# A kernel's first ten microseconds: weights asked for before the mask, and a first convolution by head pairs

## The chip, the core and the metric

The kernel runs on one core of a Trainium2 chip. A core has five engines that run side by side, each with its own list of instructions: PE (matrix products), DVE (vector operations), ACT (functions and copies), POOL (general vector operations and some DMA requests) and SP (DMA requests). They meet at semaphores. Sixteen DMA engines move data between the chip's memory and the core's SBUF, which has 128 partitions; PE writes its products to PSUM, in eight banks, from which DVE and ACT read. The metric is the device time of one execution in microseconds (us), lower is better. The time before is 713.74 us, the median of four runs (713.51, 715.17, 713.2 and 713.98).

## The reference

The input `x` has 8 sequences of 4096 tokens with 192 channels, in 8 heads of 24. A causal convolution of length 7 mixes neighbouring tokens with one softmax-normalised filter per head; a two-layer network with the activation h cos(h) follows:

```python
w = softmax(weight, axis=-1)                       # weight: [8 heads, 7 taps]
x_pad = concatenate([zeros((B, 6, D)), x], axis=1)
conv[b, s, h, g] = sum_k w[h, k] * x_pad[b, s + k, h * 24 + g]
h = conv.reshape(32768, 192) @ w_in                # w_in: [192, 2048]
out = (h * cos(h)) @ w_out                         # w_out: [2048, 192]
```

## The kernel before

**Tiling.** The 32768 tokens are 64 tasks of 512 tokens (`t` in the loop at L480); two tasks make a unit of 1024 (`u`). A unit's x is loaded as fp32 (`x_f`, L75), cast to bf16 (`x_bf`, L183), convolved on PE with banded matrices (L194), copied from PSUM to `ct` with each 64 channels twice (L207, L209, L258), and turned by a DMA transpose (L267) to `cT`, channels on partitions. Then, per task, eight blocks of the first product go to PSUM (`mm1`, L395, three `h` tiles of two banks each, used in turn), ACT takes the cosine (L402), DVE multiplies (`g`, L406), and PE adds up the second product (`mm2_step`, L439) in two further banks, `o_ps0` and `o_ps1`.

**Order.** No scheduler decides: every engine runs its instructions in the order in which the kernel writes them. From task 0 on PE's and ACT's orders are written out by hand as strings (L468 to L476), in which `h3` is the fourth block of `mm1` and `m5` five steps of the second product. Waits are put in by the framework from what the instructions read and write.

**The opening.** The lines up to L381 prepare task 0, and the change lies there.

- *The filters.* `weight` is loaded as 4 rows of 2 heads (`w_row`, L63). POOL makes `quarter` (L112 to L115), and a matmul with it (L122) spreads the four rows over the four quarters of the partitions: partitions 32q to 32q+31 hold head pair q. The softmax runs on that (L147 to L156) and ends in `wn`. Before and after this matmul, `keep_warm` has PE multiply zeros (L108).
- *The mask.* `mask[p, e, k]` is one where e + k = p + 6. POOL makes it on 32 partitions (L130, L131); DVE makes one copy to a further quarter and ACT two (L136). `prod = mask * wn` (L306) and a sum over k (L309) give `diag`: 38 columns of each band matrix.
- *The bands.* Sixteen small copies (L320; DVE, POOL and ACT by the letters "DPDPDPADPDPADPAD") put `diag` into `band`, the 8 heads' banded 128x256 matrices, which DVE has zeroed (L134). The copies go head pair by head pair.
- *Requests.* POOL asks for w_in in two halves, cast to bf16 on the way (L85), after the mask and before zeroing a row of `x_bf` (L139) and making the unit matrix `ident` (L141, L142). SP asks for x's first 512 tokens at once, and for its next ones when `diag` is done (L311 to L315).
- *First convolution and turning.* `conv_first` convolves the 512 tokens in two halves of two 128-token blocks: for each half, 8 heads by 2 (a block and the one before it), 16 matmuls of 48 columns into one bank. ACT copies out half 0, DVE half 1 (L343). Then SP asks for w_out (L96). `turn_first` turns each block on PE by a product with `ident` (L358), and ACT and DVE copy it to `cT` (L361). Task 0's first block, in two parts `h0a` and `h0b`, needs blocks 0 and 1 of `cT`, and blocks 2 and 3.
- *The second half of unit 0.* `conv_rest` convolves it during task 0 (`r` in PE's order), DVE and ACT copy it out (L207), and a DMA transpose turns it for task 1.

Of the kernel before, what the change touches and what calls it, by code (L numbers as in the profile page):

```python
# [8 lines left out]
FP32 = mybir.dt.float32  # L9
BF16 = mybir.dt.bfloat16  # L10
AF = mybir.ActivationFunctionType
ALU = mybir.AluOpType
# [4 lines left out]
def kernel(  # L17
# [66 lines left out]
    def load_w(t):  # L84
        nc.gpsimd.dma_start(out=w[64 * t : 64 * t + 64].rearrange("p k j f -> p k (j f)"), in_=w_src[t])  # L85
# [20 lines left out]
    def keep_warm(n, bank=idle):  # L106
        for _ in range(n):
            nc.tensor.matmul(out=bank, lhsT=zero[:, 0:128], rhs=zero, start=True, stop=True)  # L108
# [5 lines left out]
                            channel_multiplier=-32)  # L114
    nc.gpsimd.affine_select(out=quarter, in_=quarter, compare_op=ALU.is_ge, fill=0.0, base=31, pattern=[[-1, 128]],  # L115
                            channel_multiplier=32)
    scrap = consts.tile([128, 1], FP32)
    nc.scalar.activation(out=scrap, in_=one, func=AF.Exp)
    keep_warm(3)
# [5 lines left out]

    xb0 = xbf_pool.tile([128, UB + 1, D], BF16, name="x_bf")

    E = 32 + K - 1
    mask = consts.tile([128, E, K], BF16)
    nc.gpsimd.memset(mask[0:32], 0.0)  # L130
    nc.gpsimd.affine_select(out=mask[0:32], in_=mask[0:32], compare_op=ALU.not_equal, fill=1.0, base=1 - K,  # L131
                            pattern=[[1, E], [1, K]], channel_multiplier=-1)
    band = consts.tile([128, H, 256], BF16)
    nc.vector.memset(band, 0.0)  # L134
    for q, copy in enumerate((nc.vector.tensor_copy, nc.scalar.copy, nc.scalar.copy)):
        copy(out=mask[32 * q + 32 : 32 * q + 64], in_=mask[0:32])  # L136
    for t in range(2):
        load_w(t)
    nc.gpsimd.memset(xb0[:, 0, :], 0.0)  # L139
    ident = consts.tile([128, 128], BF16)  # L140
    nc.gpsimd.memset(ident, 0.0)  # L141
    nc.gpsimd.affine_select(out=ident, in_=ident, compare_op=ALU.not_equal, fill=1.0, base=0, pattern=[[1, 128]],  # L142
                            channel_multiplier=-1)
    wn = consts.tile([128, HQ, K], BF16)

    wmax = consts.tile([128, HQ, 1], FP32)
# [2 lines left out]
    nc.vector.tensor_tensor(out=wexp, in0=w_bc, in1=wmax.to_broadcast([128, HQ, K]), op=ALU.subtract)  # L149
    nc.scalar.activation(out=wexp, in_=wexp, func=AF.Exp)  # L150
    nc.scalar.activation(out=scrap, in_=one, func=AF.Sin)
    wsum = consts.tile([128, HQ, 1], FP32)
    nc.vector.tensor_reduce(out=wsum[:, :, 0], in_=wexp, axis=mybir.AxisListType.X, op=ALU.add)
    winv = consts.tile([128, HQ, 1], FP32)
# [56 lines left out]
    def ring_banks():  # L211
        h = h_pool.tile([128, 2, T], FP32, name="h")
        return [h[:, 0, :], h[:, 1, :]]

    def o_banks():
        return [o_pools[b].tile([128, T], FP32, name="o_ps%d" % b) for b in range(2)]
# [66 lines left out]
    def mend_edges(u):  # L283
# [12 lines left out]
        for j in (1, 2):  # L296
# [6 lines left out]
    cast_unit(0, 0, NB, nc.scalar.copy)  # L303

    prod = consts.tile([128, HQ, E, K], BF16)
    nc.vector.tensor_tensor(out=prod, in0=mask.rearrange("p (o e) k -> p o e k", o=1).to_broadcast([128, HQ, E, K]),  # L306
                            in1=wn.rearrange("p h (o k) -> p h o k", o=1).to_broadcast([128, HQ, E, K]), op=ALU.mult)
    diag = consts.tile([128, HQ, E], FP32)
    summed = nc.vector.tensor_reduce(out=diag, in_=prod, axis=mybir.AxisListType.X, op=ALU.add)  # L309
# [20 lines left out]

    def conv_first():

        banks = o_banks()
        for half in range(2):
            for h in range(H):
                for prev in range(2):
                    nc.tensor.matmul(
                        out=banks[half][:, 0 : 2 * D].rearrange("p (n k h r) -> p h n k r", n=2, k=NC, h=H)[:, h],
                        lhsT=band[:, h, 128 * prev : 128 * prev + 128],
                        rhs=bf[0][:, 2 * half + 1 - prev : 2 * half + 3 - prev, h * G : (h + 1) * G].rearrange(  # L340
                            "p n (k r) -> p n k r", k=NC),
                        start=(h == 0 and prev == 0), stop=(h == H - 1 and prev == 1), skip_group_check=True)
            m = copies[half](out=ct_tiles[0][:, 2 * half : 2 * half + 2].rearrange("p n k t w -> p (n k) t w"),  # L343
                             in_=banks[half][:, 0 : 2 * D].rearrange("p (m t w) -> p m t w", t=1, w=64).to_broadcast(
                                 [128, 2 * NC, 2, 64]))
        tc.add_manual_dep(nc.sync.nop().ins, m.ins.name, sync_dep, reason="order of the transfers")
        load_wo(0)
        load_wo(1)

    def turn_first(half):  # L350
        for n in range(2):
            last = half and n
            ps = [o_pools[0].tile([128, T], FP32, name="o_ps0")] if last else ring_banks()
            if n == 0:
                keep_warm(2 - half, ps[1])
            ps = ps[0]
            for k in range(NC):
                nc.tensor.matmul(out=ps[:, k * 128 : (k + 1) * 128],  # L358
                                 lhsT=ct_tiles[0][:, 2 * half + n, k, :, :].rearrange("p t w -> p (t w)"), rhs=ident,
                                 start=True, stop=True, skip_group_check=True)  # L360
            copies[n](out=cT[0][:, 2 * half + n].rearrange("p c k -> p (c k)"), in_=ps[:, 0 : NC * 128])  # L361
# [224 lines left out]
```

## Time and profile before

The profile is of one execution of 713.51 us; its span, from the first to the last instruction, is 711.8 us, and 1.7 us lie outside it.

| | busy us | share of the span |
|---|---|---|
| PE, matmuls | 701.2 | 99% |
| PE, weight loads | 537.2 | 75% |
| DVE | 646.6 | 91% |
| ACT | 590.4 | 83% |
| POOL | 301.3 | 42% |

In the opening, in us from the span's start:

| | from | to |
|---|---|---|
| POOL: `quarter` done | | 1.73 |
| POOL: mask | 1.73 | 3.02 |
| POOL: two requests for w_in | 2.99 | 4.43 |
| DVE: sum, reciprocal, product of the softmax (wsum to wn) | 4.17 | 4.74 |
| DVE: prod and diag | 4.78 | 6.00 |
| DVE: its seven band copies | 6.03 | 7.93 |
| PE: first convolution | 6.81 | 8.73 |
| task 0's first matmul | 10.47 | |
| DMA transpose of unit 0's second half, issue to landing | 16.69 | 21.99 |
| task 1's first matmul | 22.04 | |

A profile names groups of instructions by line, engine and tile, and tells what ended an engine's idle time before them. The chain of waits starts from the last instruction and goes back, at each step, to what released it. An engine that is idle off this chain costs nothing. The four runs shown lie 2 us apart.

### The profile page before, as it was taken

What the parts mean: (1) busy time and instruction counts of PE and PEld (TensorE: products, weight loads), DVE (VectorE), ACT (ScalarE), POOL (GpSimd) and SP (SyncE); (2) the same over time, 40 slices, a digit from 0 to 9 for tenths busy, and PEclk for the clock granted to TensorE, in tenths of its full rate; (3) what the DMA queues carried; (4) which work ended last, traced back from release to release, by engine and by line L of the source; (5) the groups of instructions that cost most, each with busy time, mean ns of one, the idle gap of its engine ahead of it and who ended that gap; (6) DMA issues with size and microseconds to landing.
All of it is one profiled execution on the core that took longest, in us unless ns stands there. A gap on an engine that the chain in (4) does not pass through costs nothing.

```text
span 711.8 us, 26520 instructions
## 1 busy us (share of the span) xinstructions
PE 701.2 (99%) x11829; PEld 537.2 (75%) x11829; DVE 646.6 (91%) x601; ACT 590.4 (83%) x719; POOL 301.3 (42%) x307
## 2 busy tenths in 40 slices
PE   7899999999999999999999999999999999999997
PEld 3577777777777777777777777777777777777776
DVE  7899999999999999999999999999999999999995
ACT  7888888888888888888888888888888888888774
POOL 6653335553235543445542255534355532453200
PEclk9999999999999999999999999999999999999999
DMA  8963553444653544543546544545535555513402
GB/s 214 236 145 81 141 146 102 119 118 102 147 126 107 133 99 121 146 121 101 144 86 136 145 107 114 128 92 145 147 82 138 104 117 145 126 50 91 96 25 68
DMA packets 183713, 85.25 MB, mean 120 GB/s; under 512 B 111664, under 2 KB 183216, under 8 KB 183600
## 3 DMA queue, kind: packets, MB, share of 16 engines
q1 hardware_dynamic: 182888, 82.59, 47.8%
q8 instruction: 92, 1.51, 0.8%
q0 software_dynamic: 416, 0.79, 0.7%
q14 instruction: 21, 0.17, 0.1%
q10 hardware_dynamic: 296, 0.20, 0.1%
HBM read 31.36 MB, written 25.17 MB: 79 GB/s over the span
## 4 chain that ended last, share of the span: by engine, by line
PE 96%; DVE 1%; DMA 1%; ACT 1%; issue 0%; POOL 0%; POOLq 0%; SPq 0%
PE o_ps L439 47%; PE h L395 46%; PE h L194 3%; DMA cT<-ct 1%; DVE g L406 0%; ACT cs L402 0%; PE h L439 0%; DVE band L320 0%; POOL mask L131 0%; ACT mask L136 0%; ACT ct L343 0%; PE o_ps L194 0%; DVE diag L309 0%; DVE cT L361 0%; PE h L358 0%
## 5 line engine op out<-in xcount | busy, mean ns | idle before, releaser
L406 DVE TENSOR_TENSOR g<-h,cs 128x1024 bf16<-128x1024 f32 (+1 forms) x513 | 606.2, 1220 | 30.4 <-ACT cs L402 19.8
L402 ACT ACTIVATE cs<-h 128x1024 bf16<-128x1024 f32 (+1 forms) x513 | 512.0, 1026 | 100.1 <-PE h L395 66.0
L439 PEld LDWEIGHTS <-g 64*128 64x128 bf16 x8192 | 368.9, 94 | 90.8 <-SPq L167 0.6
L439 PE MATMUL o_ps<-wo,g 64*128 64x192 bf16 x8128 | 434.3, 243 | 0.2 <-SPq L167 0.2
L395 PE MATMUL h<-cT,w 64*128 64x512 bf16 (+1 forms) x3078 | 412.4, 376 | 4.1 <-DVE g L406 2.1
L395 PEld LDWEIGHTS <-w 64*128 64x128 bf16 x3078 | 160.7, 94 | 71.6 <-issue 4.0
L292 POOL TENSOR_TENSOR edge_prod<-cT,tap 128x1008 f32<-128x1008 bf16 x30 | 67.2, 2241 | 346.4 <-DMA cT<-ct 346.4
L183 POOL CAST x_bf<-x_f 128x1728 bf16<-128x1728 f32 (+2 forms) x33 | 80.6, 2444 | 5.8 <-DMA x_f<-in_x_dram 5.4
L209 ACT CAST ct<-h 128x384 bf16<-128x384 f32 x120 | 51.7, 482 | 8.5 <-PE h L194 4.9
L450 DVE COPY o_sb<-o_ps 128x384 f32<-128x384 f32 x63 | 35.2, 558 | 23.6 <-PE o_ps L439 23.2
L258 POOL COPY ct<-ct 128x1536 bf16<-128x1536 bf16 (+1 forms) x31 | 45.7, 1473 | 2.4 <-ACT ct L209 2.4
L194 PE MATMUL h<-x_bf,band 64*128 64x192 bf16 (+1 forms) x472 | 41.0, 243 | 0.0
L297 POOL TENSOR_TENSOR edge_prod<-edge_prod 128x144 f32<-128x144 f32 x60 | 33.4, 556 | 4.7
L295 POOL TENSOR_TENSOR edge_prod<-edge_prod 128x432 f32<-128x432 f32 x30 | 30.4, 1012 | 2.4
L450 ACT COPY o_sb<-o_ps 128x384 f32<-128x384 f32 x63 | 29.8, 473 | 1.6 <-PE o_ps L439 1.6
L194 PEld LDWEIGHTS <-band 64*128 64x128 bf16 (+1 forms) x496 | 24.7, 94 | 2.1 <-issue 1.0
L298 POOL TENSOR_TENSOR cT<-edge_prod 128x144 bf16<-128x144 f32 x30 | 18.3, 610 | 2.4
L260 POOL COPY ct<-x_bf 128x192 bf16<-128x192 bf16 x60 | 19.2, 349 | 0.0
L108 PE MATMUL o_ps<-zero 128*128 128x512 bf16 x12 | 4.2, 508 | 1.3 <-DVE zero L103 1.3
L460 DVE COPY o_sb<-h 128x192 f32<-128x192 f32 x1 | 0.4, 359 | 3.7 <-PE h L439 3.7
L108 PEld LDWEIGHTS <-zero 128*128 128x128 bf16 x15 | 1.5, 115 | 2.9 <-DVE zero L103 1.3
L460 ACT COPY o_sb<-h 128x192 f32<-128x192 f32 x1 | 0.3, 319 | 3.8 <-PE h L439 3.8
(62 smaller groups left out, 43.8 us busy)
## 6 DMA issues: line engine op xcount, KB each, us to landing
out_dram<-o_sb SPq DMA_DIRECT2D x63, 384.0 KB
x_f<-in_x_dram SPq DMA_DIRECT2D x30, 768.0 KB
x_f<-in_x_dram SPq DMA_DIRECT2D x31, 96.0 KB
x_f<-in_x_dram SPq DMA_DIRECT2D x4, 384.0 KB
wo_f<-in_moe_w_out_dram SPq DMA_DIRECT2D x4, 384.0 KB
w<-in_moe_w_in_dram POOLq DMA_DIRECT2D x2, 384.0 KB, 6.2
cT<-ct SPq DMA_TRANSPOSE x32
out_dram<-o_sb ACTq DMA_DIRECT2D x2, 96.0 KB
```

Source lines behind the costliest of these rows:

```text
L183: copy(out=bf[u][:, n0 + o : n1 + o, :].rearrange("p n (h k r) -> p (n h) k r", k=NC, r=R), in_=x_tiles[u][:, n0:n1, :].rearrange("p n (h ...
L194: return nc.tensor.matmul(out=ps[i // 2][:, 0 : (n1 - n0) * 2 * G].rearrange("p (n k i r) -> p i n k r", n=n1 - n0, k=NC, i=2)[:, i % 2], ...
L209: copy(o[:, :, 0, :], i[:, :, 0, :])
L258: nc.gpsimd.tensor_copy(out=ct[:, 0:nb, :, 1, :], in_=ct[:, 0:nb, :, 0, :])
L292: nc.gpsimd.tensor_tensor(out=edge_prod, in0=window, in1=tap.rearrange("p (a b k) -> p a b k", a=1, b=1).to_broadcast([128, NC * UB, K - 1 ...
L295: nc.gpsimd.tensor_tensor(out=edge_prod[:, :, :, 0:3], in0=edge_prod[:, :, :, 0:3], in1=edge_prod[:, :, :, 3:6], op=ALU.add)
L297: nc.gpsimd.tensor_tensor(out=edge_prod[:, :, :, 0], in0=edge_prod[:, :, :, 0], in1=edge_prod[:, :, :, j], op=ALU.add)
L395: nc.tensor.matmul(out=h[:, i, n0 * 128 : n1 * 128], lhsT=w[rows, k, j, :], rhs=c[rows, m0 + n0 : m0 + n1, k, :], start=(k == 0), stop=(k ...
L402: nc.scalar.activation(out=cs[:, :, part], in_=h[:, :, part], func=AF.Sin, bias=math.pi / 2.0, scale=1.0)
L406: nc.vector.tensor_tensor(out=g_tiles[t][:, 2 * j : 2 * j + 2, part], in0=h[:, :, part], in1=cs[:, :, part], op=ALU.mult)
L439: ms.append(nc.tensor.matmul(out=o_ps[tt, b, si], lhsT=g_tiles[tt][rows, f, s * 128 : (s + 1) * 128], rhs=wo[rows, f // 2, f % 2, :], star ...
L450: copies[b](o_sb[t][:, 2 * b : 2 * b + 2, :].rearrange("p s d -> p (s d)"), o_ps.pop((t, b)))
```

## The change

Five things change, all before task 0:

- `load_w`, the two requests for w_in, goes from behind the mask to directly behind `quarter` on POOL.
- The 3-dimensional mask goes. POOL makes `shifted`, 128 rows of a unit matrix shifted by six columns. `ident` becomes a view of it. The first 32 rows by 44 columns of it are copied to the four quarters of `rows32` (POOL quarters 1 and 2, DVE 0 and 3), and `mask` becomes a view of `rows32` in which rows overlap: element (e, k) is column e + k. ACT's two mask copies and DVE's one go. DVE's two new copies stand behind the softmax's subtraction and before its sum.
- `conv_first` runs by head pairs instead of by halves: for each pair the four blocks one after the other, each into its own bank (`o_ps0`, `o_ps1` and the two banks of one `h` tile). 64 matmuls of 24 columns take the place of 32 of 48.
- Each block is copied out singly, ACT blocks 0 and 2, DVE 1 and 3.
- `turn_first` takes its banks in another order, and two of the three warming matmuls there go. The three `h` tiles are used as often as before.

The tiles that are allocated after these constants, x's among them, begin 416 bytes lower in each partition.

```diff
@@ -114,6 +114,8 @@
                             channel_multiplier=-32)
     nc.gpsimd.affine_select(out=quarter, in_=quarter, compare_op=ALU.is_ge, fill=0.0, base=31, pattern=[[-1, 128]],
                             channel_multiplier=32)
+    for t in range(2):
+        load_w(t)
     scrap = consts.tile([128, 1], FP32)
     nc.scalar.activation(out=scrap, in_=one, func=AF.Exp)
     keep_warm(3)
@@ -125,22 +127,20 @@
 
     xb0 = xbf_pool.tile([128, UB + 1, D], BF16, name="x_bf")
 
-    E = 32 + K - 1
-    mask = consts.tile([128, E, K], BF16)
-    nc.gpsimd.memset(mask[0:32], 0.0)
-    nc.gpsimd.affine_select(out=mask[0:32], in_=mask[0:32], compare_op=ALU.not_equal, fill=1.0, base=1 - K,
-                            pattern=[[1, E], [1, K]], channel_multiplier=-1)
+    shifted = consts.tile([128, 128 + K - 1], BF16)
+    nc.gpsimd.memset(shifted, 0.0)
+    nc.gpsimd.affine_select(out=shifted, in_=shifted, compare_op=ALU.not_equal, fill=1.0, base=1 - K,
+                            pattern=[[1, 128 + K - 1]], channel_multiplier=-1)
+    ident = shifted[:, K - 1 :]
     band = consts.tile([128, H, 256], BF16)
     nc.vector.memset(band, 0.0)
-    for q, copy in enumerate((nc.vector.tensor_copy, nc.scalar.copy, nc.scalar.copy)):
-        copy(out=mask[32 * q + 32 : 32 * q + 64], in_=mask[0:32])
-    for t in range(2):
-        load_w(t)
+
+    E = 32 + K - 1
+    rows32 = consts.tile([128, E + K - 1], BF16)
+    mask = bass.AP(rows32.tensor, rows32.offset, [rows32.ap[0], [0, HQ], [1, E], [1, K]])
+    for q in (1, 2):
+        nc.gpsimd.tensor_copy(out=rows32[32 * q : 32 * q + 32], in_=shifted[0:32, 0 : E + K - 1])
     nc.gpsimd.memset(xb0[:, 0, :], 0.0)
-    ident = consts.tile([128, 128], BF16)
-    nc.gpsimd.memset(ident, 0.0)
-    nc.gpsimd.affine_select(out=ident, in_=ident, compare_op=ALU.not_equal, fill=1.0, base=0, pattern=[[1, 128]],
-                            channel_multiplier=-1)
     wn = consts.tile([128, HQ, K], BF16)
 
     wmax = consts.tile([128, HQ, 1], FP32)
@@ -149,6 +149,8 @@
     nc.vector.tensor_tensor(out=wexp, in0=w_bc, in1=wmax.to_broadcast([128, HQ, K]), op=ALU.subtract)
     nc.scalar.activation(out=wexp, in_=wexp, func=AF.Exp)
     nc.scalar.activation(out=scrap, in_=one, func=AF.Sin)
+    for q in (0, 3):
+        nc.vector.tensor_copy(out=rows32[32 * q : 32 * q + 32], in_=shifted[0:32, 0 : E + K - 1])
     wsum = consts.tile([128, HQ, 1], FP32)
     nc.vector.tensor_reduce(out=wsum[:, :, 0], in_=wexp, axis=mybir.AxisListType.X, op=ALU.add)
     winv = consts.tile([128, HQ, 1], FP32)
@@ -303,7 +305,7 @@
     cast_unit(0, 0, NB, nc.scalar.copy)
 
     prod = consts.tile([128, HQ, E, K], BF16)
-    nc.vector.tensor_tensor(out=prod, in0=mask.rearrange("p (o e) k -> p o e k", o=1).to_broadcast([128, HQ, E, K]),
+    nc.vector.tensor_tensor(out=prod, in0=mask,
                             in1=wn.rearrange("p h (o k) -> p h o k", o=1).to_broadcast([128, HQ, E, K]), op=ALU.mult)
     diag = consts.tile([128, HQ, E], FP32)
     summed = nc.vector.tensor_reduce(out=diag, in_=prod, axis=mybir.AxisListType.X, op=ALU.add)
@@ -330,30 +332,31 @@
 
     def conv_first():
 
-        banks = o_banks()
-        for half in range(2):
-            for h in range(H):
-                for prev in range(2):
-                    nc.tensor.matmul(
-                        out=banks[half][:, 0 : 2 * D].rearrange("p (n k h r) -> p h n k r", n=2, k=NC, h=H)[:, h],
-                        lhsT=band[:, h, 128 * prev : 128 * prev + 128],
-                        rhs=bf[0][:, 2 * half + 1 - prev : 2 * half + 3 - prev, h * G : (h + 1) * G].rearrange(
-                            "p n (k r) -> p n k r", k=NC),
-                        start=(h == 0 and prev == 0), stop=(h == H - 1 and prev == 1), skip_group_check=True)
-            m = copies[half](out=ct_tiles[0][:, 2 * half : 2 * half + 2].rearrange("p n k t w -> p (n k) t w"),
-                             in_=banks[half][:, 0 : 2 * D].rearrange("p (m t w) -> p m t w", t=1, w=64).to_broadcast(
-                                 [128, 2 * NC, 2, 64]))
+        banks = o_banks() + ring_banks()
+        for q in range(4):
+            for n in range(NB):
+                for h in range(HQ * q, HQ * (q + 1)):
+                    for prev in range(2):
+                        nc.tensor.matmul(
+                            out=banks[n][:, 0:D].rearrange("p (k h r) -> p h k r", k=NC, h=H)[:, h],
+                            lhsT=band[:, h, 128 * prev : 128 * prev + 128],
+                            rhs=bf[0][:, n + 1 - prev, h * G : (h + 1) * G].rearrange("p (k r) -> p k r", k=NC),
+                            start=(h == 0 and prev == 0), stop=(h == H - 1 and prev == 1), skip_group_check=True)
+        for n in range(NB):
+            m = copies[n % 2](out=ct_tiles[0][:, n],
+                              in_=banks[n][:, 0:D].rearrange("p (m t w) -> p m t w", t=1, w=64).to_broadcast([128, NC, 2, 64]))
         tc.add_manual_dep(nc.sync.nop().ins, m.ins.name, sync_dep, reason="order of the transfers")
         load_wo(0)
         load_wo(1)
 
     def turn_first(half):
+        banks = o_banks() if half else None
         for n in range(2):
-            last = half and n
-            ps = [o_pools[0].tile([128, T], FP32, name="o_ps0")] if last else ring_banks()
-            if n == 0:
-                keep_warm(2 - half, ps[1])
-            ps = ps[0]
+            ps = banks[n] if half else ring_banks()
+            if not half:
+                if n == 0:
+                    keep_warm(1, ps[1])
+                ps = ps[0]
             for k in range(NC):
                 nc.tensor.matmul(out=ps[:, k * 128 : (k + 1) * 128],
                                  lhsT=ct_tiles[0][:, 2 * half + n, k, :, :].rearrange("p t w -> p (t w)"), rhs=ident,
```

## The prediction, before the result was known

> **What bounds the kernel.** I read the page first, then PE's waits by stretch, then the chain of waits up to 23 us, then each engine's timeline and the DMA share there.
>
> ```profile
> span 711.8 us, 26520 instructions
> ...
> PE 701.2 (99%) x11829; PEld 537.2 (75%) x11829; DVE 646.6 (91%) x601; ACT 590.4 (83%) x719; POOL 301.3 (42%) x307
> ```
>
> PE is busy 99% of the span, and the table of PE's waits from 40 us to the end is empty: there the order of matmuls is fixed and PE never stops. So the change, which touches the first 11 us alone, is worth exactly the shift of the moment from which PE runs without stop. The chain shows what sets that moment (start us, length us, what):
>
> ```profile
> 2.06 0.97 POOL mask L131
> ...
> 3.06 0.41 ACT mask L136
> ...
> 3.48 0.41 ACT mask L136
> ...
> 4.17 0.18 DVE wsum L153
> ...
> 4.78 0.49 DVE prod L306
> ...
> 5.29 0.72 DVE diag L309
> ...
> 8.07 0.27 PE o_ps L337 x4
> ...
> 8.36 0.81 ACT ct L343
> ...
> 9.76 0.57 DVE cT L361
> ...
> 10.47 0.67 PE h L395 x6
> ...
> 16.69 5.30 DMA cT<-ct
> ...
> 22.04 0.82 PE h L395 x6
> ```
>
> The reader should see two stretches. To 10.47 a chain of small steps: mask, softmax, band, first convolution, turning. From 11.2 to 22 DVE and ACT run task 0 (DVE is idle for 0.64 us at most between 11.79 and 23.33), then the DMA transpose of unit 0's second half, issued at 16.69, holds PE until 22.04. ACT's line says how much of that a faster transpose could give:
>
> ```profile
> 22.90 4.29 ACT L402 ACTIVATE cs<-h 128x1024 bf16<-128x1024 f32 x4 [0.82 <-PE h L395]
> ```
>
> ACT had ended task 0's last cosine at 22.08; only 0.82 us of the wait is the transpose's alone. Last, the DMA engines by stretch (columns: busy time of PE, PEld, DVE, ACT, POOL, then the clock, DMA share, GB/s):
>
> ```profile
> 3.80:4.80 1.00, 1.00 (x5) 0.33 (x3) 0.53 (x4) 0.96 (x3) 1.00 (x3) 1.00 0.36 33
> 4.80:9.20 4.40, 3.10 (x40) 1.58 (x38) 3.35 (x10) 3.50 (x7) 1.99 (x8) 1.00 0.99 148
> ...
> 10.20:18.40 8.20, 6.56 (x70) 3.40 (x69) 7.10 (x10) 7.04 (x11) 5.64 (x7) 1.00 1.11 323
> ...
> 20.20:21.70 1.50, 0.16 (x2) 0.00 (x0) 1.23 (x1) 1.50 (x4) 0.49 (x1) 1.00 1.01 230
> ```
>
> From 4.8 to 18.4 the DMA engines are full. The DMA records say with what: x's first block moves from 1.95 to 3.74, w_in's packets from 4.49 to 10.26; x's next blocks, asked for from 6.02, move nothing before 9.2, and x and w_out then fill the engines to about 18.5, with stragglers to 20. The transpose's packets run from 18.1 to 21.4 in the middle of that, with a hole.
>
> **Part 1, POOL's order.** Today: `quarter` to 1.73, mask memset and select to 3.02, the two w_in issues 2.99 to 4.43 (0.81 and 0.63), then x_bf memset, ident memset 0.22 and select 0.50. After: w_in issues 1.73 to 3.17; `shifted` memset, 0.23 by ident's row (134 columns for 128), a gap of 0.08, select 0.52: ready at 4.00. So the mask's source comes 0.98 later than today's 3.02, all of it the 1.44 of the issues less 0.46 of cheaper making. Behind it on POOL: two rows32 copies, 0.24 each by the band-copy row, to 4.5, then the x_bf memset to 4.8, which nobody needs before the first matmul at 6.8; POOL's first band copy at 6.1 stays free.
>
> **Part 2, mask copies.** Gone: ACT's two (0.41 each) and DVE's one (0.22). ACT's exponential no longer stands behind them: it goes from 3.92 to 3.74 (the subtraction ends at 3.72), and with it the table load and the x cast, 0.18 earlier; x_bf was ready at 6.75 and the last band at 7.93, so this is off the path. But DVE now waits for `shifted` in front of wsum: two 32x44 copies of 0.17 (between a 14-wide operation at 0.17 and the 32x266 copy at 0.22), 4.03 to 4.37; wsum starts at 4.39 instead of 4.17: +0.22. prod starts near 5.0, and POOL's rows, done at 4.5, don't hold it. prod and diag are the same in elements (0.48, 0.71); the overlapping view reads the same rows of seven. Bounds of this step: -0.1 (both issues at 0.63, copies 0.1 each) to +0.5 (DVE's and POOL's copies one after the other).
>
> [...]
>
> The band copies keep order and price, so the last lands at 7.93 + 0.22 = 8.15.
>
> **Part 3, convolution.** 64 matmuls of 24 columns replace 32 of 48. Start to start they stand 25 ns apart today (20 in 0.48), set by something other than 48 columns; I take 25 ns, bounds 12 and 30. A head pair is 16, 0.40. Pairs 0 to 2 go as their bands come (today 6.81, 7.2, 7.61), so the last pair starts when its band allows, at 8.29 against 8.07, and block 0 ends after its first four, as half 0 does today. Evacuation starts at 8.58 against 8.36: no gain, and no loss.
>
> **Part 4, evacuation.** One copy of 768 per engine (ACT 0.80, DVE 0.96) becomes two of 384 (0.48 and 0.56, as the L361 rows of that size). Blocks 2 and 3 are halves of one `h` tile, and in the built program DVE's copy of block 3 waits for ACT's copy of block 2; nothing like it was there before. ACT: block 0 at 8.58 to 9.06, block 2 to 9.57. DVE: block 1 8.69 to 9.25, idle, block 3 9.59 to 10.15, then block 1's turned copy 10.17 to 10.73. PE's first task matmul needs that: 10.88 instead of 10.47. Without the wait it would be 10.55. The fewer warming matmuls were beside waits and cost nothing; the clock column is 1.00 in all stretches, and PE keeps working in each 2 us here.
>
> **Part 5, w_in earlier.** Today the second weight load of task 0 starts 0.15 after the first matmul, when w_in's second half lands (last packet 10.26); six matmuls take 0.65 where two steps of 0.107 and the last one's 0.27 would be about 0.5. After, w_in is in by about 9.4: -0.15. So task 0's first cosine moves by 0.41 - 0.15 = +0.25 (bounds: -0.4 with the low mask and no wait of block 3, +0.6 with the high mask and half of the 0.15).
>
> **Part 6, the DMA queue.** w_in's packets move from 1.26 earlier, where the engines had room (share 0.36 from 3.8 to 4.8). x's first block could lose its tail: it ends at 3.74 and isn't read before 5.35, so even 1 us is covered. SP issues x's next blocks 0.22 later (they wait for diag) and w_out at 10.15 instead of 9.73 (behind the last copy of Part 4), both covered: the engines are still on w_in at 6.2, and on x's 1.28 MB (at 323 GB/s, from about 8.4) until 12.3. So everything behind w_in comes about 1.1 earlier and w_out's backlog ends near 17.3. The transpose is issued after DVE's copies, at 16.69 + 0.25 = 16.94, into a nearly empty queue. Its price there: later ones of 27 blocks begin 1.2 after the issue and move packets for 4.4, 0.163 a block, and this one landed 0.6 after its last packet; 12 blocks make 1.2 + 2.0 + 0.6 = 3.8 instead of 5.3. Bounds 3.8 and 5.3. At 3.8 it lands at 20.7 and is no longer waited for: late next is ACT (22.08 + 0.25), then DVE's last product, which frees the h buffer for task 1's third block. The 0.82 of ACT's idle is what can be had: 0.25 - 0.82 = -0.57. x for unit 2 and the second transpose follow the same queue and shift at least as far; the edge copy behind that one ended at 33.14 for a matmul at 33.39, so it must shift too.
>
> **Sum.** -0.55 on the profiled execution of 713.51 (span 711.8 and 1.7 around it): 712.96. The median, 713.74, stands 0.23 above that execution: 713.2.
>
> **Rivals.**
> (a) The transfer relief isn't had: the transpose has a hole of its own (DMA share 0.15 from 19.4 to 20.2, when nearly all of w_out had gone), which speaks for it; that later ones show none speaks against. Then only the opening counts: +0.25, 714.0; with the high bound +0.6, 714.4.
> (b) The opening gains: the mask 0.1 late only, block 3 not held (10.55 less 0.12), w_in's 0.15 in full: -0.2 - 0.82, 712.7. The wait in the built program speaks against.
> (c) Slower by one mechanism: POOL. Every us that the two issues and `shifted` take longer is a us on wsum. With the relief had, it turns the sign when the opening is 0.82 late, that is when `shifted` is ready at 4.6; to 0.2% it needs 6.0, twice the 1.44 seen and more. Price at 5.0: +0.4, 714.2.
> (d) The main loop changes: the smaller constants move all large tiles down by 416 bytes, from multiples of 64 bytes to 32 beyond. 0.2% would be 0.13 ns on each of 11270 task matmuls. The rows with such an address already (band's weight loads 95 ns, w's 94) show nothing.
>
> **How the numbers follow.** 0.2%, 1.4 us, is about what a measurement of this kernel can tell from no change; the four runs shown lie 2 us apart. The sum 0.45, (a) 0.2, (b) 0.2, (c) 0.08, (d) 0.07, split evenly by sign. The sum reads as faster beyond 0.2% in one of six by the runs' scatter, (b) in half, (d) half: 0.2. Slower beyond: (c) half, (d) half, a little of (a): 0.1. Range: (b) less the 0.5 that the lowest run lies below the median, 712.2 (its low bound, -1.2, lies inside); (a) at its high bound and a little, 714.6.
>
> **What would show it.** Right: `shifted` ready near 4.0, wsum near 4.4, DVE idle before block 3's copy, first task matmul near 10.9 with no wait for w, transpose under 4.5 and no PE wait on it. Wrong: a transpose still over 5 us, prod waiting on POOL, or any PE wait after 40 us.

## The result and the profile after

The changed kernel takes 715.68 us (median; 714.41 to 717.19) where the kernel before takes 713.49 on the same chips: the ratio is 1.0027, 95% interval 1.0022 to 1.0032. It is slower by 0.27%, 1.9 us (the medians lie 2.2 apart). The forecast was 713.2, within 712.2 to 714.6.

The profile is of an execution of 715.25 us. From its page:

```profile
span 713.6 us, 26581 instructions
...
PE 702.6 (98%) x11859; PEld 538.3 (75%) x11859; DVE 646.6 (91%) x603; ACT 589.2 (83%) x718; POOL 300.3 (42%) x307
```

PE has 30 more matmuls and 30 more weight loads: 32 of each in the first convolution, less two warming matmuls. Their busy time is 1.4 us more. From 40 us on PE again waits for nothing, so the whole difference must have arisen before, and it can be read off one mark: when DVE starts the k-th product (`g`) of the main loop, here minus before.

| product | before | after | shift |
|---|---|---|---|
| first, task 0 | 11.79 | 13.25 | +1.47 |
| ninth, the last of task 0 | 22.11 | 23.58 | +1.46 |
| tenth, the first of task 1 | 23.96 | 24.72 | +0.76 |
| fourteenth | 28.86 | 29.55 | +0.70 |
| sixteenth | 32.05 | 33.59 | +1.54 |
| last | 701.49 | 703.02 | +1.53 |

Three steps: 1.47 late at the start, 0.7 won back at 24 us, 0.8 lost again at 30 us. Each has its row in PE's waits from 8 to 60 us (us in total, times, longest):

```profile
PE h L398 <- DVE g L409: 2.4, 6, 0.6
PE o_ps L442 <- SPq L169: 1.3, 1, 1.3
PE h L398 <- DMA w<-in_moe_w_in_dram: 0.9, 1, 0.9
PE h L398 <- DMA cT<-ct: 0.4, 1, 0.4
```

The transpose's wait, 1.7 before, is 0.4: the step won. The transpose did not land earlier for that: issued 1.47 later (18.16 for 16.69), it lets PE go on at 22.21, where before PE went on at 22.04. The wait for w_in is new. The wait for SP at L169 was 0.2. L169 is the no-operation by which SP orders two halves of PE's second product (`Turn.mark`).

**The start.** The engines' timelines (start us, busy us, what; POOL, then DVE, then PE):

```profile
3.41 0.29 POOL L132 TENSOR_SCALAR_AFFINE_SELECT shifted<-shifted 128x134 bf16<-128x134 bf16 x1
...
4.12 0.17 DVE L155 TENSOR_REDUCE wsum<-wexp 128x2 f32<-128x14 f32 x1
...
9.80 0.56 DVE L346 CAST ct<-h 128x384 bf16<-128x384 f32 x1 [0.23 <-ACT ct L346]
...
10.97 0.27 PE L398 MATMUL h<-cT,w 64*128 64x256 bf16 x1 [0.21 <-DVE cT L364]
12.09 1.26 PE L398 MATMUL h<-cT,w 64*128 64x256 bf16 x15 [0.86 <-DMA w<-in_moe_w_in_dram]
```

The mask is not late: `shifted` is ready at 3.70, wsum starts 0.05 earlier than before, the last band lands at 7.94 (7.92). DVE's 0.23 before block 3 is the wait that was forecast. The first task matmul stands at 10.97 for 10.47, and the second, 0.15 behind it before, is now 1.12 behind: w_in's second half has not landed. 0.50 and 0.97 make the 1.47. But the second matmul goes by w_in alone: it follows 0.05 behind the landing of w_in's second half, at 12.04 (10.58 before), so the 0.50 is hidden behind that landing.

**The requests.** The stretches that the prediction showed, with the same columns:

```profile
3.80:4.80 1.00, 1.00 (x4) 0.30 (x2) 0.78 (x5) 0.98 (x2) 0.66 (x3) 1.00 0.91 125
4.80:9.20 4.40, 4.25 (x71) 2.33 (x69) 3.13 (x10) 2.83 (x7) 1.46 (x6) 1.00 1.01 129
...
10.20:18.40 8.20, 6.10 (x63) 3.28 (x64) 6.11 (x10) 5.61 (x10) 4.69 (x6) 1.00 1.10 304
```

The engines are busier from 3.8 to 4.8, as forecast (0.91 for 0.36), but from 4.8 to 9.2 they move less than before, 129 GB/s for 148, at the same share. The DMA records: w_in's packets run from 3.32 to 11.00 (start of the first, start of the last, here and below), where before they ran from 4.49 to 10.08, and a packet takes 244 ns on average where it took 217. Asked for 1.3 us earlier, w_in ends 0.9 later.

**The end of the chain.** Where the chain of waits before ran through the mask, the convolution and the transpose, it now comes by another way (start us, length us, what):

```profile
10.79 7.76 DMA wo_f<-in_moe_w_out_dram
18.68 1.48 POOL wo L92
20.70 5.39 DMA x_f<-in_x_dram
26.23 2.57 POOL x_bf L185
28.80 2.35 SPq L269
```

The last row is SP, busy with the second DMA transpose (unit 1's), and then PE at 31.26. Timelines of SP and PE there:

```profile
24.34 6.81 SPq L269 DMA_TRANSPOSE cT<-ct  x1
...
29.72 0.20 PE L280 MATMUL h<-wn,pick 128*128 128x7 bf16 x2
31.26 0.58 PE L442 MATMUL o_ps<-wo,g 64*128 64x192 bf16 x10 [1.34 <-SPq L169]
```

SP's no-operation stands behind the issue of the transpose, and PE's next matmul behind the no-operation. Before, that issue ran from 22.89 to 29.30, and PE lost 0.2. By stretches (DMA share and GB/s last), after:

```profile
28.00:29.00 1.00, 1.00 (x16) 0.62 (x12) 1.00 (x2) 0.51 (x1) 0.85 (x2) 1.00 0.97 211
29.00:30.00 1.00, 0.92 (x14) 0.56 (x8) 0.78 (x2) 1.00 (x2) 1.00 (x1) 1.00 2.06 69
```

and before:

```profile
29.00:30.00 1.00, 0.79 (x15) 0.55 (x13) 1.00 (x2) 1.00 (x3) 1.00 (x1) 1.00 1.27 289
30.00:31.00 1.00, 0.87 (x12) 0.56 (x13) 1.00 (x2) 0.57 (x4) 1.00 (x1) 1.00 2.50 225
31.00:32.00 1.00, 1.00 (x21) 0.69 (x17) 0.21 (x1) 1.00 (x2) 0.15 (x1) 1.00 0.07 7
```

For about a microsecond little moves (from 29 us after, from 30.7 before), and the DMA engines are counted busy twice over in the stretch where it begins. The DMA records show what stands ahead of it: a single packet of 16384 bytes on an instruction queue, at 28.78 after and at 30.29 before; 0.4 us later some twenty of the transpose's 256-byte packets, whose median is 18 ns, take 1.3 to 1.4 us each. After, this falls inside the transpose's issue, and SP can't end it; before, the issue was over.

### The profile page after: what moved, and what is told of

The parts are those of the page before. It is cut to its first block, busy times and chain, and to the rows that moved or that the text cites. A ratio compares the mean times of both kernels' runs of the same rounds, so it can differ in the third digit from the quotient of the medians.

```text
span 713.6 us, 26581 instructions
## 1 busy us (share of the span) xinstructions
PE 702.6 (98%) x11859; PEld 538.3 (75%) x11859; DVE 646.6 (91%) x603; ACT 589.2 (83%) x718; POOL 300.3 (42%) x307
## 4 chain that ended last, share of the span: by engine, by line
PE 95%; DMA 2%; DVE 1%; POOL 1%; SPq 0%; ACT 0%; issue 0%; POOLq 0%; DVEq 0%
PE o_ps L442 47%; PE h L398 45%; PE h L196 3%; DMA wo_f<-in_moe_w_out_dram 1%; DMA x_f<-in_x_dram 1%; PE h L442 0%; POOL x_bf L185 0%; SPq L269 0%; POOL wo L92 0%; PE o_ps L108 0%; DVE g L409 0%; DVE band L322 0%; ACT cs L405 0%; PE o_ps L340 0%; ACT ct L346 0%
```

## Experiments

They ask three things: which part costs (e1 to e4), whether the 16384-byte pieces do it (e7, e8, e10), and why w_in is late (e9, e13). e5, e6, e11 and e12 move other transfers. Where a ratio is given, it is to the kernel before on the same chip, with its 95% interval.

### One part undone: e1 to e4

e1 asks for w_in behind the copies of the rows, at 2.72 instead of 1.68.

```diff
-    for t in range(2):
-        load_w(t)
     scrap = consts.tile([128, 1], FP32)
...
         nc.gpsimd.tensor_copy(out=rows32[32 * q : 32 * q + 32], in_=shifted[0:32, 0 : E + K - 1])
+    for t in range(2):
+        load_w(t)
```

> The changed kernel, with the two w_in requests moved behind the rows32 copies, so that they are issued near 2.9 us as in the kernel before. Theory A (asked for early, w_in's tail mixes with x's next blocks and lands at 12.0 instead of 10.6; that is the loss): the 0.86 us wait of the first task matmul goes or falls under 0.2 us, DVE's first product moves from 13.25 to about 12.4, ratio to the kernel before about 1.000 to 1.001. Rival B (the convolution in single blocks costs it): the wait for w_in goes, but the ratio stays above 1.0015.

e2 keeps early w_in and mask, with `conv_first` and `turn_first` as before (their lines of the diff undone). e3 is both: only the mask and the addresses are changed.

> The changed kernel, with the first convolution, its copies and the turning as in the kernel before; w_in still early, mask still a view. Theory A: w_in still lands near 12.0 and holds the first task matmul, now for about 1.4 us (the matmul is ready near 10.5), ratio 1.002 to 1.003. Rival B: ratio near 1.000.

> Only the mask as a view and the identity matrix as a view are left of the change; w_in's requests and the convolution as before. Both theories: no difference to the kernel before, ratio 0.9990 to 1.0005; diag ends within 0.1 us of 6.0. A ratio above 1.001 would speak for the mask or for the lower addresses of the large tiles.

e4 is the changed kernel with x's next requests held until the last band copy:

```diff
-    tc.add_manual_dep(nc.sync.nop().ins, summed.ins.name, sync_dep, reason="order of the transfers")
-    load_unit(0, NB, UB)
...
-        three[k](out=band[...], in_=diag[...])
+        put = three[k](out=band[...], in_=diag[...])
+    tc.add_manual_dep(nc.sync.nop().ins, put.ins.name, sync_dep, reason="order of the transfers")
+    load_unit(0, NB, UB)
```

> The changed kernel, with SP's requests for x's next blocks held until the last band copy (7.95 instead of 6.05). Theory A: w_in's packets end near 10 instead of 11.2, its landing near 10.4, no wait for w_in at the first task matmul, DVE's first product near 12.4; x's later blocks come about 1 us later, which may show behind; ratio 1.000 to 1.002. Rival A2 (w_in's own packets are slow when asked for early, whatever x does): it still lands past 11.5 and the wait stays.

Measured:

| | ratio | w_in's packets, us | PE's wait for w_in | for SP near 30 us |
|---|---|---|---|---|
| e1, w_in late | 1.0015 [1.0005, 1.0024] | 4.24 to 9.79 | none | 1.63 |
| e2, convolution as before | 1.0002 [0.9993, 1.0012] | 3.54 to 9.85 | 0.2 | 0.35 |
| e3, mask alone | 1.0005 [0.9995, 1.0014] | 4.25 to 9.82 | none | 0.34 |
| e4, x held | 1.0041 [1.0026, 1.0056] | 3.51 to 10.61 | none | 1.76 |

The mask and the shift of addresses show no cost (e3; its interval ends at 0.14%). Undoing the early request wins back about half (e1), and the other half is the convolution's, but not in the opening: in e1 the first product stands at 11.83, as before (11.79), and only then does PE wait 1.63 for SP. The wait for SP goes with the new convolution: 1.3 to 1.8 in the three kernels that have it, 0.35 or less where the old one stands. e2 misses what theory A expected, a loss of 0.2 to 0.3% with early w_in alone; e9 comes back to it. e4 speaks against x's next blocks as what delays w_in: held back 2.6 us, they left w_in's end at 10.61. (PE did not wait for w_in there because its first task matmul stood at 11.67; in that profile the whole opening stood 0.7 later.) Its own loss is x, which PE then waited 1.6 for.

### The instruction stream: e7, e8 and e10

The instruction queue with the 16384-byte pieces moves 92 of them in the profile before and 93 after. For PE's 23658 and 23718 matmuls and weight loads that is 257 and 255 to a piece, so they are taken for PE's instructions. The new convolution puts 60 more instructions into the opening. e7 adds 60 to the kernel before, and nothing else:

```diff
-    keep_warm(9)
+    keep_warm(7)
+    for _ in range(32):
+        nc.tensor.matmul(out=idle[:, 0:24], lhsT=zero[:, 0:128], rhs=zero[:, 0:24], start=True, stop=True)
```

> The kernel before, with 60 more instructions on PE in the opening: two of the nine warming matmuls after the weights' row are replaced by 32 matmuls of 24 columns each, on the same bank of zeros. They end before the bands are ready, so nothing waits for them. Theory F (PE's instructions come by DMA in pieces of 16384 bytes, and a piece that comes while the transposition of unit 1 is being issued holds its packets for about 1.4 us, SP with it, and PE's second product of task 1 behind SP): the piece seen at 30.29 comes at 28.3 to 29.0, inside the issue; the issue takes 7.0 to 7.8 us instead of 6.41; PE waits 1.0 to 1.8 us on SP near 29.5; ratio 1.0010 to 1.0025. Theory G (the rest of the new convolution, its banks, its four evacuations and its later opening, makes the loss of the convolution part): PE's wait on SP stays at 0.2 to 0.4, ratio 1.000 within 0.0007.

e8 is the opposite: the changed kernel, with two blocks per matmul.

```diff
-        banks = o_banks() + ring_banks()
+        banks = o_banks()
         for q in range(4):
-            for n in range(NB):
+            for half in range(2):
                 for h in range(HQ * q, HQ * (q + 1)):
                     for prev in range(2):
...
-                            rhs=bf[0][:, n + 1 - prev, ...
+                            rhs=bf[0][:, 2 * half + 1 - prev : 2 * half + 3 - prev, ...
...
         for n in range(NB):
             m = copies[n % 2](out=ct_tiles[0][:, n],
-                              in_=banks[n][:, 0:D]...
+                              in_=banks[n // 2][:, n % 2 * D : (n % 2 + 1) * D]...
```

> The changed kernel, with the first convolution still by head pairs and still evacuated block by block, but with two blocks of 48 columns in one bank as before: 32 matmuls instead of 64, so PE's stream is as long as before (4 instructions shorter). Theory F: the piece of instructions comes at 30 or later, the second transposition's issue takes 5.8 to 6.5 us, PE's wait on SP is at most 0.4; what is left is the opening and w_in's late landing, ratio 0.9998 to 1.0012. Theory G: the four evacuations and the order by head pairs are still there, ratio 1.0018 to 1.0030, wait on SP 1.0 or more.

e10 is e8 with e1's later request.

> The changed kernel with both suspects taken out: w_in asked for behind the copies of the rows, and two blocks in one bank, so PE has no more instructions than before. What stays of the change is the mask by view, the order by head pairs and the evacuation block by block. If the 60 instructions and the early requests are all that costs: ratio 0.9995 to 1.0005, no wait of PE over 0.4 on SP or on w_in, first product of VectorE at 11.6 to 12.0. If the evacuation block by block or the order by head pairs costs too: 1.0008 or more.

e7 measured 1.0022 [1.0011, 1.0032]. The 32 matmuls hold up nothing (half 0 is copied out at 8.33, before at 8.36; first product at 11.92 for 11.79). The piece comes at 28.79 instead of 30.29. SP's timeline, PE's waits and the stretch, in this order:

```profile
23.00 7.65 SPq L269 DMA_TRANSPOSE cT<-ct  x1
```

```profile
PE o_ps L441 <- SPq L169: 1.6, 1, 1.6
```

```profile
29.00:30.00 1.00, 0.17 (x4) 0.07 (x1) 1.00 (x2) 1.00 (x3) 1.00 (x1) 1.00 1.90 72
```

The issue is 1.25 longer than before's 6.40, the stretch is down to 72 GB/s, and PE waits 1.6. Sixty instructions that nothing waits for cost that much 20 us later.

e8 measured 1.0014 [1.0003, 1.0024], above the range by a little: no wait for SP over 0.25 is left, the piece comes at 32.05 and the issue takes 5.51, but w_in's last packet is at 10.81 and PE waits 1.1 for it. What comes with that wait stands in the next stretches (the granted clock is the third number from the end):

```profile
11.00:12.00 1.00, 0.05 (x2) 0.06 (x4) 0.00 (x0) 0.00 (x0) 0.00 (x0) 0.79 1.09 303
12.00:13.00 1.00, 1.00 (x12) 0.68 (x14) 0.00 (x0) 0.20 (x1) 0.03 (x1) 0.50 1.09 327
13.00:14.00 1.00, 1.00 (x8) 0.72 (x6) 0.57 (x1) 0.96 (x2) 1.00 (x1) 0.50 1.13 303
14.00:15.00 1.00, 1.00 (x8) 0.62 (x5) 0.76 (x2) 0.32 (x2) 0.93 (x5) 0.51 1.10 273
```

From 11.58 to 14.99 PE runs at half its clock. e10 measured 0.9992 [0.9983, 1.0002], no loss left, and no wait over 0.25 for either:

```profile
22.87 6.07 SPq L269 DMA_TRANSPOSE cT<-ct  x1
```

The runs make a table of two causes:

| | w_in asked for late | early |
|---|---|---|
| PE's stream as long as before | e10 0.9992, e3 1.0005 | e8 1.0014, e2 1.0002 |
| 60 instructions more | e1 1.0015, e7 1.0022 | the change 1.0027 |

Against e10, the early request alone costs 0.0022 (e8) and the 64 matmuls for 32 alone 0.0023 (e1): 1.6 us each. Both together cost 0.0035, 2.5 us, less than the sum. The intervals are some 0.001 to either side.

These ratios mix two kinds of execution, with and without such a stretch of half clock. Between PE's warming and its last matmuls the traces have eight of them (two in e5 and in e12, one in e6, e8, e9 and e11). Each is 3.41 us long and begins inside a wait of PE of 0.7 to 3.8 us or at most 1.0 us behind one. Not every such wait brings one: the changed kernel's profile, with waits of 0.9 and 1.3, has none. An execution with one shows a mean clock of about 0.998, and the mean clock is on record for executions without a trace too:

| | executions | with half clock | median of the others | less before's |
|---|---|---|---|---|
| before | 73 | 16 | 713.36 | |
| e3, mask alone | 10 | 2 | 713.28 | -0.08 |
| e10, neither | 11 | 2 | 713.13 | -0.23 |
| e8, early request | 11 | 6 | 713.83 | +0.47 |
| e2, early request | 10 | 0 | 714.04 | +0.68 |
| e1, 64 matmuls | 10 | 1 | 714.48 | +1.12 |
| e7, 60 instructions | 8 | 2 | 715.10 | +1.74 |
| the change | 42 | 18 | 715.34 | +1.98 |
| e13, further below | 10 | 0 | 712.77 | -0.59 |

At full clock the two causes add up: 0.70 (e8) and 1.35 (e1) above e10 make 2.05, and the change stands 2.21 above it. The rest of e8's 1.6 us goes with the half clock, which more than half of its executions have. The groups are small, and where the stretch fell is on record only for executions with a trace. With half clock the kernel before takes 715.28 and the changed one 716.45 (medians).

As e10 still evacuates block by block and goes by head pairs, these show no cost.

### Why w_in is late: e9 and e13

By its ratio e2's early request costs nothing; its median, 714.04, stands 0.68 above that of the kernel before beside it (713.36). e9 is the same kernel again, for another profile.

> The same kernel as in e2 (early requests for w_in, mask by view, convolution as before) once more, for another profiled execution. e2's profile ends 0.7 us ahead of before's while its median does not. Theory W (w_in asked for early lands late in most executions, and by how much differs from one to the next): the last w_in packet later than e2's 9.85, at 10.3 to 11.0, the second task matmul 0.6 to 1.5 behind the first, time 713.6 to 714.6. If the landing of w_in is steady: last packet at 9.7 to 10.0, second matmul within 0.3 of the first, time 712.7 to 713.1, and the median of e2 has another cause.

This one execution took 716.96, more than was expected and more than any of e2's ten (712.86 to 714.48); e2's profiled one was the fastest of them. w_in's packets ran from 3.52 to 10.52, and the second task matmul stood 1.63 behind the first. In that execution the first transpose was late as well (PE waited 2.0 for it), and the clock was halved from 24.80 to 28.21. So the early request's last packet differs between executions of one kernel by 0.67 us and its landing by 1.4 (10.67 in e2, 12.06 here), and e2's profile is a lucky one.

Over the profiles, the packets of an early request start at 3.3 to 3.7 and end at 9.85 to 11.01 (seven profiles); those of a later one start at 4.2 to 4.5 and end at 9.79 to 10.16 (seven). From first to last that is 6.3 to 7.7 us for the early ones and 5.5 to 5.6 for the later ones. x's first block ends at 3.8 to 4.0, between the two. e13, which starts from e8, asks for one of its four blocks, so that it ends at 2.56. The other three are left out and filled with 0.5, so this kernel doesn't compute the reference's output:

```diff
-    load_unit(0, 0, NB)
+    load_unit(0, 0, 1)
...
     nc.vector.memset(band, 0.0)
+    nc.vector.memset(x_tiles[0][:, 1:NB, :], 0.5)
```

> e8 (two blocks in one bank, w_in asked for early) with only one of the four blocks of x's first request loaded from DRAM; VectorE fills the other three with 0.5, so the output is not the reference's in unit 0's first blocks, and all later work is the same. x's first request then ends near 2.6 instead of 3.9, before w_in's first packet at 3.3. Theory X (w_in lands late because its first packets move beside the end of x's first block, which leaves its work uneven): last w_in packet at 8.8 to 9.6, second task matmul within 0.3 of the first, ratio 0.9980 to 0.9998 against e8's 1.0014. If w_in is late for another reason (asked for early in itself, x's next blocks): last packet at 10.3 to 11.0, second matmul 0.6 to 1.5 behind the first, ratio 1.0008 to 1.0020.

It measured 0.9982 [0.9972, 0.9992]. w_in's packets run from 3.20 to 8.76, the second task matmul follows the first at once. The stretches of e8:

```profile
8.00:9.00 1.00, 0.68 (x11) 0.41 (x12) 0.12 (x1) 0.64 (x2) 0.00 (x0) 1.00 0.83 110
9.00:10.00 1.00, 0.75 (x10) 0.45 (x10) 1.00 (x3) 0.70 (x2) 0.00 (x0) 1.00 0.84 199
10.00:11.00 1.00, 0.56 (x4) 0.21 (x4) 0.89 (x2) 0.48 (x1) 0.00 (x0) 1.00 1.13 221
```

and of e13, where x's next blocks have the engines from 8 us on:

```profile
8.00:9.00 1.00, 0.67 (x12) 0.39 (x12) 0.10 (x1) 0.61 (x2) 0.00 (x0) 1.00 1.06 298
9.00:10.00 1.00, 0.75 (x10) 0.45 (x11) 1.00 (x3) 0.72 (x2) 0.00 (x0) 1.00 1.09 361
10.00:11.00 1.00, 0.72 (x12) 0.43 (x13) 0.91 (x2) 0.48 (x1) 0.42 (x1) 1.00 1.08 353
```

PE's waits in e13 up to 24 us:

```profile
PE h L401 <- DVE g L412: 1.8, 5, 0.6
PE h L401 <- DMA cT<-ct: 0.4, 1, 0.4
```

With the overlap gone, the request can be early, and all that the prediction hoped for is there: w_in 1.3 earlier, the first transpose's wait 0.4, the tenth product 0.72 earlier than before and the last 0.70. (Later, PE waits 0.6 for SP at 29 us: the piece comes at 28.82, just before the issue ends at 28.91.) e13 also moves 0.3 MB less, but that isn't what makes w_in quick: from first packet to last it takes 5.6 us, as the later requests do that meet no other load at their start. In e8 the engines are busy 0.83 and 0.84 of the time in the two microseconds before 10, not full, while w_in is not in. What the overlap does inside the engines isn't shown: the records don't name the engine of a packet, and that an uneven rest is left to a few of them was only the author's guess.

### Other transfers moved: e5, e6, e11, e12

e5 moves the loads of unit 3 from ahead of the second transpose to behind it, in the changed kernel; e6 does so in the kernel before.

```diff
             cast_wo(1)
-            load_unit(3)
-            load_edges(3)
             cast_unit(2)
...
                 if t == 1:
                     turn_unit(1)
+                    load_unit(3)
+                    load_edges(3)
```

> The changed kernel, with the loads of unit 3 of x (and its edge rows) asked for behind the second transposition instead of ahead of it. Theory F in its part on SP (the second transposition's long issue is what holds SP's no-operation and so PE): with 0.8 MB less in the queue ahead of it the issue takes 4 to 5.5 us, ends by 29.0 even with a piece of instructions in it, PE's wait on SP falls under 0.4, ratio 1.0005 to 1.0015 instead of 1.0027. Rival: the issue is as long as ever, since its own packets set it, and only starts at the same time: 1.002 to 1.003. A cost of the move would show as a wait for the cast of unit 3 after 45 us.

> The kernel before, with the same move of unit 3's loads behind the second transposition. There is only 0.2 us of wait on SP to be had, but the second transposition should land earlier. If PE's row of work to 34 us is held by the transposition's landing or by SP: ratio 0.9985 to 0.9997. If both are hidden there: 1.0000 within 0.0006.

e12 also puts POOL's edge copy of unit 1 ahead of its cast of unit 3, and e11 does both to the kernel before and asks for w_out's second half behind the first transpose.

```diff
                 if t == 1:
-                    cast_unit(3)
                     mend_edges(1)
+                    cast_unit(3)
```

```diff
         load_wo(0)
-        load_wo(1)
...
                         turn_unit(0, NB, UB)
+                        load_wo(1)
```

> e5 without its new wait: the changed kernel with unit 3's loads behind the second transposition, and POOL's edge copy of unit 1 ahead of its cast of unit 3 (in e5 the copy stood behind that cast, and PE waited 3.8 us for it). No wait for POOL's copy; PE's wait on SP 0.4 to 0.8 as in e5 instead of 1.34; the early w_in still costs its 0.6 to 1.1. Ratio 1.0010 to 1.0022 instead of 1.0027. If SP's wait is not what the 60 instructions cost, 1.0024 or more.

> A try at a faster kernel: before, with the second half of w_out asked for behind the first transposition instead of ahead of it, unit 3's loads behind the second, and the edge copy ahead of the cast of unit 3. The relief of the first transposition without the early w_in: it lands 0.5 to 1.5 earlier, PE's wait on it falls from 1.68 to 0.4 to 1.0, nothing waits for w_out's second half before 26 us, ratio 0.9983 to 0.9994. If x of unit 2, now 0.6 MB further back in the queue, holds POOL's cast and the second transposition, the gain is given back: 0.9997 to 1.0012.

All four are slower than what they start from: e5 1.0105 [1.0091, 1.0119], e6 1.0050 [1.0037, 1.0064], e12 1.0077 [1.0063, 1.0092], e11 1.0062 [1.0050, 1.0074]. Behind their long waits the clock is halved for 3.41 us in each of the four profiles (from 37.4 to 39.8 us on), and PE runs slower there. The waits of e5 name the reason, the copy on POOL that stood behind the cast of unit 3:

```profile
PE h L398 <- POOL cT L288: 3.8, 1, 3.8
...
PE o_ps L442 <- SPq L169: 0.6, 1, 0.6
```

and with that copy moved, in e12, the convolution of unit 3 itself needs the cast at 36 us:

```profile
PE h L196 <- POOL x_bf L185: 2.8, 1, 2.8
...
PE o_ps L442 <- SPq L169: 0.5, 1, 0.5
```

Unit 3's x cannot come later. On SP the issue takes 4.7 us in both and the wait falls from 1.34 to 0.5 in e12, as expected, and to 0.6 in e5, where under 0.4 was expected. In e11 the first transpose lands earlier without early w_in (tenth product 0.67 earlier than before), but x of unit 2 comes behind w_out: PE waits for it 1.9 at 28 us and for unit 3's 2.7 at 35. No variant with the whole computation beats the kernel before by more than its interval; e10 comes nearest.

## Why the prediction was wrong, step by step

**Right.** PE's row has no wait after 40 us, so all is decided in the first 40; the reading of the kernel holds. Block 3's copy waits for ACT (Part 4): 0.23. The engines had room from 3.8 to 4.8. The first transpose (Part 6) costs what was forecast: PE goes on 4.05 after its issue instead of 5.35. But 0.70 won for a forecast 0.82 is luck here, since the transpose landed no earlier and task 0 was 1.47 late; in e13, with the opening as before, the relief is there as forecast (issued at 16.67, PE goes on at 20.78).

**Part 2, the mask +0.22 late: wrong, with no effect.** The select of 128x134 took 0.29, not 0.52: it was priced by `ident`'s row (0.50 for 128 columns), a select that ran beside DVE's prod; whether that made it long isn't shown. POOL's and DVE's copies ran side by side (3.77 to 4.24 and 3.74 to 4.09), not one after the other as at the upper bound. With that term gone the opening should have been better than forecast.

**Part 3, the convolution "no gain, and no loss": wrong in two terms.** The 25 ns held. Block 0's evacuation began at 8.91 in this profile, 0.55 later than half 0's before, but at 8.35 and 8.36 in e5 and e12, which have the same opening. The nine warming matmuls explain it: they took 4.02 us in the profile after and 2.77 in e5's, and the convolution's first matmul came at 7.40 and 6.73, the task's first at 10.97 and 10.41. From 7.40 the 64 matmuls ran back to back to 9.00, and the bands, by which the forecast timed the pairs, no longer set the pace. The old convolution stands such a late warming without loss: in e2, e9 and e11 its first matmul also came at 7.40, and the task's first at 10.44 to 10.49. The forecast took one execution's warming for the kernel's. In this profile the 0.50 is hidden behind w_in.

The warming's length goes with the clock. The clock column reads 1.00 in all of these stretches, but the traces have no clock record ahead of the first full clock. That record begins at 4.62 before, at 7.55 after and at 4.59 in e5. Before, the warming matmuls start 427 ns apart ahead of it and 216 behind it; after, all nine start ahead of it, 427 apart. What sets the moment at which the full clock begins isn't shown.

What was missed altogether is that 64 matmuls for 32 are 60 more instructions to fetch. They were priced by PE's time alone; 60 more in the stream of the kernel before cost 1.6 us (e7).

**Part 5, w_in in by 9.4, -0.15: wrong by the most.** The last packet began at 11.00, 0.92 later than before, and w_in landed 1.46 later (12.04); the second task matmul fell back by 0.97 against the first, where a gain of 0.15 was forecast. The step that failed is in Part 6: of the overlap with x's first block it asked what x would lose, and found that covered. It never asked what w_in would lose. e13 shows that w_in, without the overlap, is in at 8.76 (landed at 9.27). One reading is off without effect: x's first block ends at 3.83 in the trace before, not at 3.74.

**Part 6, "x for unit 2 and the second transpose follow the same queue and shift at least as far": wrong.** Nothing behind w_in came 1.1 earlier, as w_in itself ended later: POOL's first casts of x's next blocks and of w_out, which wait for these transfers, began at 13.13 and 18.68, 1.2 and 1.3 later than before. The second transpose's issue began 1.45 later and ended 1.86 later. The 0.70 won at the first transpose was lost again at SP's no-operation, 0.2 us of wait that the chain before didn't show and whose slack was not asked about.

**Rivals.** None named the mechanism. (a), no relief, would have been 714.0 to 714.4, but the transpose did take less; (b), the opening gains, worked out at 712.7, is not what e13 shows with 712.78: there the first product stands at 11.77, as before, and the gain is the transpose's. (c) put a loss on POOL, which was early. (d), at its 0.2%, is excluded by e3.

**The sum put right**, for the profiled execution: +1.47 to the first product, all of it w_in's landing, -0.70 at the first transpose, +0.77 at SP's no-operation, and 0.2 in the last task after the last product: +1.74 for 713.51, 715.25.

## What to carry to other kernels

A request moved earlier must be priced against what is still moving when its first packets start, in both directions: what it takes from the other, and what it loses: here w_in, asked for 1.3 us earlier, was in 0.9 later. A loop split into more and smaller instructions lengthens the engine's instruction stream, and with it a later fetch can shift, as here from 30.29 to 28.79 us by 60 instructions (e7); look where the next one falls, and whether a long DMA issue, and a semaphore behind that issue on the same queue, stand there. A gain at one wait counts only as far as the next queue in line has slack, so read the short waits (0.2 us here) around it as well as the long one. And before medians are compared, look at the mean clock of each execution: here executions with one stretch of half clock take 1 to 2 us more, as much as the change costs.

## What the runs showed of the hardware

- Behind one 16384-byte instruction piece a running DMA transpose moved little for about a microsecond. In the stretch from 29 to 30 us the kernel before and e10 move 289 and 305 GB/s; the changed kernel and e7, whose pieces come at 28.78 and 28.79, move 69 and 72. Some twenty of the transpose's packets, whose median is 18 ns, take 1.3 us before and 1.4 after. 92 pieces for 23658 matmuls and weight loads (before) and 93 for 23718 (after) are about 256 instructions a piece. PE has no wait there but the one for SP, behind the transpose's issue (1.34 us after, 1.6 in e7).
- The piece moved with the number of instructions ahead of it: 60 more moved the second one from 30.29 to 28.79 (e7). With a stream as long as before it came at other times too: at 29.09 in e3 and at 32.05 in e8.
- The last packet of w_in, cast on its way by POOL's requests, began at 9.85 (e2) to 11.01 us from the span's start when its first packets met x's first block (11.00 in the profile after), at 9.79 (e1) to 10.16 when they came up to 1.2 us later (10.08 in the profile before), and at 8.76 when x's block was already through (e13).
- The issue of the second DMA transpose occupied SP for 4.66 us in e12 and 7.65 in e7 (6.40 before, 6.81 after); what stood behind it on SP waited, a no-operation too (31.19 in the profile after, behind an issue that ended at 31.15).
- PE's granted clock fell to half for 3.41 us eight times in these traces (two in e5 and in e12, one in e6, e8, e9 and e11; from 11.58 to 14.99 in e8), each time inside a wait of PE of 0.7 to 3.8 us or at most 1.0 us behind it.
